# Batched decode attention with an MLP: four kv heads per K/V tile (16 KB runs), regrouped score rows, P transposed by VectorE

## Chip, core, metric

One core of a Trainium2 chip. Time is device microseconds (us) of one execution, the median of several runs. The kernel before takes 207.43 us (207.33 to 207.88). "Ratio" below is the mean time of a kernel's fast runs over the mean of the kernel before's fast runs of the same rounds, so it is not quite the quotient of the medians quoted beside it. A run over 1.5% above the fastest of its kernel counts as slow and is left out of ratios.

## The reference, cut to what matters

```
# A: one decode step, B=8, D=512, 32 q heads, 8 kv heads, window W=2048 of 8192 keys, Dh=128, bf16
q = (layernorm(x) @ wq)                                # wq: 512 x 4096
k, v = k_cache[:, :, Sk-W:, :], v_cache[:, :, Sk-W:, :] # [b, head] -> 2048 x 128, 4 q heads share one
o = softmax(q k^T * Dh**-0.5) v
h = x + o @ wo                                         # wo: 4096 x 512
# B: a second layernorm, a residual MLP (w3: 512 x 1792, w4: 1792 x 512, gelu); S=1 makes its token shift zero
out = h + B(layernorm(h))
```

K and V of the window are 64 pieces of 512 KB each, one per batch and kv head: together 67.1 MB of the 79.2 MB that the program reads. Each byte is used for very little arithmetic, so I expected the transfer from memory to be the limit; the page below shows it as such (DMA engines over 90% busy, 408 GB/s).

With the given inputs the attention term `o @ wo` has a root mean square of 6.6e-5 beside 1.05 for the output. A comparison of outputs can therefore not see an error in the attention. So the programs were also executed functionally, off the chip, on larger inputs (K, V and wq times 20, wo times 157) whose attention term is 0.30.

## The kernel before

K and V of one (batch, kv head) are one transfer of 512 KB. Partition `p` gets rows `16p` to `16p+15`, a contiguous run of 4 KB:

```python
NC = W // 128                                   # 16 rows per partition
knat = sb([128, NK, NC * DH], dt.bfloat16, "knat")   # 15 slots; vnat: 16 slots
...
e.dma_start(knat[:, ks, :].rearrange("p (c d) -> p c d", c=NC),
            A_k_cache[b, g, W0:SK, :].rearrange("(p c) d -> p c d", c=NC)).then_inc(sem_k[ks], 16)
```

TensorE transposes K in 128x128 pieces into PSUM, ScalarE and VectorE copy halves to SBUF (`Elo`, `Ehi`), TensorE forms scores (rows: 32 heads in each of four key quarters), and per batch P is transposed by four TensorE transposes and one VectorE copy. Then PV:

```python
for q in range(4):
    for jt in range(4):
        c = 4 * q + jt
        ins = e.matmul(misc[:, OT4.start + q*H + R*g : OT4.start + q*H + R*(g+1)],
                       vnat[:, vs, c*DH:(c+1)*DH], pT_sb[:, b % 2, c, R*g:R*(g+1)],
                       start=(jt == 0), stop=(jt == 3))
```

All transfers go through SyncE's one queue: x, wq (4 MB), K and V interleaved, wo, w3, w4.

## Time and profile before

| | before | view |
|---|---|---|
| DMA engines busy | over 90% in nearly all slices up to 200 us | forty slices |
| rate, 40 to 160 us | 408 GB/s | table by stretches |
| TensorE busy | 78% of the span | first part of the page |
| end | last weights land at 200.0 us, then 3.3 us of matmuls | chain of waits |

Lines of the page of the kernel before. Each digit of the PEclk and DMA rows, and each number of the GB/s row, is one fortieth of the span; the packets line says how many packets the transfers became:

```profile
span 205.6 us, 6282 instructions
PE 161.1 (78%) x2744; PEld 123.5 (60%) x2744; DVE 83.4 (41%) x197; ACT 81.8 (40%) x101; POOL 3.0 (1%) x13
...
PEclk9999997975997599769696969579969588885556
DMA  6999999999999999999999999999999999999980
GB/s 206 440 388 416 409 408 410 409 408 407 405 411 408 407 410 409 406 409 410 406 410 406 408 409 410 407 406 408 409 406 408 410 410 381 356 393 340 398 305 22
DMA packets 24250, 79.59 MB, mean 387 GB/s; under 512 B 2192, under 2 KB 6304, under 8 KB 24096
...
q1 hardware_dynamic: 24224, 79.19, 97.9%
```

The DMA row is full and flat at about 408 GB/s: the stream is the limit. The count "under 512 B 2192": these are the 4-byte packets (2192 records, median 9 ns) that go with a transfer's landing, 16 for each K or V transfer. I read them as one for each engine that the transfer used, because the packets in flight agree: 16.3 on average between 40 and 160 us here.

The table by stretches (one row, 40 to 160 us: busy us of each engine and its instructions, granted clock, DMA share, GB/s):

```profile
40.00:160.00 120.00, 104.59 (x1741) 80.65 (x1740) 54.82 (x122) 52.37 (x62) 0.00 (x0) 0.83 1.03 408
```

The end of the chain of waits (start us, duration us, what):

```profile
187.19 12.79 DMA knat<-in_B_w_dram
199.98 0.14 issue
200.12 3.30 PE b L689 x28
```

### The profile page before, as it was taken

To read this page: it belongs to the slowest core of one execution; us is meant where nothing else is said; L and a number is where in the kernel's file an instruction comes from. 1 tells how busy PE (TensorE), PEld (TensorE's weight loads), DVE (VectorE), ACT (ScalarE), POOL (GpSimd) and SP (SyncE) were. 2 spreads that over 40 slices of the span, in tenths; PEclk is the share of its full clock that TensorE was granted. 3 is DMA by queue.
4 is the path that set the end of the run, shared out by engine and by line. 5 is a ranking of instruction groups with operands and counts; after the bars stand their busy time and mean duration, and the time that the engine had idled before them with its cause. 6 is when DMAs were issued, how large, how long until landed. Compare 5 with 4: busy or idle time off the path is not lost.

```text
span 205.6 us, 6282 instructions
## 1 busy us (share of the span) xinstructions
PE 161.1 (78%) x2744; PEld 123.5 (60%) x2744; DVE 83.4 (41%) x197; ACT 81.8 (40%) x101; POOL 3.0 (1%) x13
## 2 busy tenths in 40 slices
PE   1039957799779977995899699698996698775645
PEld 0039745487548754873688468575884576565542
DVE  5103534624562356234454444347345253351120
ACT  3203846514641464145523561157145341350040
POOL 5000000000000000000000000000000000000000
PEclk9999997975997599769696969579969588885556
DMA  6999999999999999999999999999999999999980
GB/s 206 440 388 416 409 408 410 409 408 407 405 411 408 407 410 409 406 409 410 406 410 406 408 409 410 407 406 408 409 406 408 410 410 381 356 393 340 398 305 22
DMA packets 24250, 79.59 MB, mean 387 GB/s; under 512 B 2192, under 2 KB 6304, under 8 KB 24096
## 3 DMA queue, kind: packets, MB, share of 16 engines
q1 hardware_dynamic: 24224, 79.19, 97.9%
q8 instruction: 22, 0.36, 0.7%
q14 instruction: 4, 0.03, 0.0%
HBM read 79.18 MB, written 0.01 MB: 385 GB/s over the span
## 4 chain that ended last, share of the span: by engine, by line
DMA 54%; SPq 24%; PE 18%; issue 2%; DVE 0%
DMA knat<-in_A_k_cache_dram 48%; SPq L239 12%; PE kT_ps L385 10%; SPq L249 7%; DMA knat<-in_B_w_dram 6%; SPq L259 4%; PE misc L523 3%; PE S_ps L415 2%; PE b L689 2%; SPq L277 1%; PE b L470 0%; PE misc L443 0%; PE b L504 0%; PE misc L475 0%; DVE out_sb L699 0%
## 5 line engine op out<-in xcount | busy, mean ns | idle before, releaser
L396 ACT ACTIVATE kT_sb<-kT_ps 128x1024 bf16<-128x1024 bf16 x64 | 65.4, 1023 | 87.7 <-PE kT_ps L385 87.6
L385 PE MATMUL kT_ps<-ident_b,knat 128*128 128x128 bf16 x1024 | 84.6, 249 | 19.6 <-DMA knat<-in_A_k_cache_dram 18.6
L385 PEld LDWEIGHTS kT_ps<-ident_b,knat 128*128 128x128 bf16 x1024 | 72.4, 113 | 36.9 <-DMA knat<-in_A_k_cache_dram 27.8
L403 DVE COPY kT_sb<-kT_ps 128x1024 bf16<-128x1024 bf16 x64 | 44.2, 691 | 61.9 <-PE kT_ps L385 61.9
L523 PE MATMUL misc<-pT_sb,vnat 128*128 128x4 bf16 x1024 | 29.0, 165 | 3.1 <-issue 1.6
L523 PEld LDWEIGHTS misc<-pT_sb,vnat 128*128 128x128 bf16 x1024 | 27.4, 98 | 6.6 <-issue 4.2
L415 PE MATMUL S_ps<-kT_sb,qblk 128*32 128x512 bf16 x256 | 29.0, 446 | 0.3 <-DVE kT_sb L403 0.3
L415 PEld LDWEIGHTS S_ps<-kT_sb,qblk 128*32 128x32 bf16 x256 | 6.6, 95 | 8.8 <-issue 3.3
L357 PE MATMUL S_ps<-xlnT,wbig 128*128 128x8 bf16 x128 | 3.6, 168 | 6.5 <-DMA wbig<-in_A_wq_dram 6.5
L436 ACT ACTIVATE P_sb<-S_ps,negmcol 128x512 bf16<-128x512 f32 x8 | 5.5, 687 | 7.2 <-DVE negmcol L428 7.2
L533 DVE TENSOR_TENSOR prod_sb<-misc,w_sb 128x128 f32<-128x128 f32 x8 | 2.3, 292 | 14.7 <-PE misc L523 14.7
L509 DVE COPY w_sb<-b 128x128 f32<-128x128 f32 x8 | 2.3, 292 | 13.5 <-PE b L504 13.5
L357 PEld LDWEIGHTS S_ps<-xlnT,wbig 128*128 128x128 bf16 x128 | 3.5, 104 | 6.5 <-issue 6.5
L426 DVE TENSOR_REDUCE mcol<-S_ps 128x1 f32<-128x512 f32 x8 | 5.5, 682 | 0.6 <-PE S_ps L415 0.6
L581 ACT ACTIVATE std<-var,eps_t 128x8 f32<-128x8 f32 x1 | 0.3, 301 | 12.4 <-DVE var L632 12.4
L373 DVE TENSOR_SCALAR qblk<-S_ps 128x32 bf16<-128x32 f32 x8 | 0.9, 182 | 9.8 <-PE S_ps L357 9.8
L504 PE MATMUL b<-w_row,ones_row 1*128 1x128 f32 x16 | 4.7, 385 | 0.0
L460 ACT ACTIVATE a_row<-d_row 1x128 f32<-1x128 f32 x8 | 2.5, 306 | 5.7 <-DVE d_row L453 5.7
L443 PE MATMUL misc<-ident_f,mcol 128*1 128x128 f32 x16 | 3.8, 328 | 1.0 <-DVE negmcol L428 1.0
L599 PE MATMUL S_ps<-oT_all,wbig 128*128 128x8 bf16 x128 | 3.7, 168 | 0.7 <-DMA wbig<-in_A_wo_dram 0.7
L599 PEld LDWEIGHTS S_ps<-oT_all,wbig 128*128 128x128 bf16 x128 | 3.6, 104 | 0.8 <-DMA wbig<-in_A_wo_dram 0.8
L659 PE MATMUL misc<-uT,knat 128*128 128x8 bf16 x56 | 1.7, 168 | 2.7 <-DMA knat<-in_B_w_dram 2.7
(78 smaller groups left out, 70.0 us busy)
## 6 DMA issues: line engine op xcount, KB each, us to landing
knat<-in_A_k_cache_dram SPq DMA_DIRECT2D x64, 512.0 KB, 15.6
vnat<-in_A_v_cache_dram SPq DMA_DIRECT2D x64, 512.0 KB, 15.8
wbig<-in_A_wq_dram SPq DMA_DIRECT2D x1, 4096.0 KB, 12.3
wbig<-in_A_wo_dram SPq DMA_DIRECT2D x1, 2048.0 KB, 19.9
knat<-in_B_w_dram SPq DMA_DIRECT2D x1, 1792.0 KB, 12.3
wbig<-in_A_wo_dram SPq DMA_DIRECT2D x1, 1024.0 KB, 12.3
wbig<-in_A_wo_dram SPq DMA_DIRECT2D x2, 512.0 KB, 11.2
knat<-in_B_w_dram SPq DMA_DIRECT2D x1, 1024.0 KB, 12.8
```

What stands on the lines that cost most here:

```text
L239: e.dma_start(vnat[:, vs, :].rearrange("p (c d) -> p c d", c=NC), A_v_cache[b, g, W0:SK, :].rearrange("(p c) d -> p c d", c=NC),).then_inc ...
L249: e.dma_start(knat[:, ks, :].rearrange("p (c d) -> p c d", c=NC), A_k_cache[b, g, W0:SK, :].rearrange("(p c) d -> p c d", c=NC),).then_inc ...
L259: e.dma_start(wo_v[:, h0:h1, :], A_wo[h0 * 128:h1 * 128, :].rearrange("(h p) n -> p h n", p=128)).then_inc(sem_wo[j], 16)
L357: ins = e.matmul(S_ps[:, 0, h * B:(h + 1) * B], wq_v[:, kc, h * DH:(h + 1) * DH], xlnT[:, kc * B:(kc + 1) * B], start=(kc == 0), stop=(kc ...
L385: ins = e.matmul(buf[:, c * 128:(c + 1) * 128], knat[:, ks, c * DH:(c + 1) * DH], ident_b[:, :], is_transpose=True)
L396: e.activation(kT_sb[:, i % NKT, 0:W // 2], kT_ps[i % 2][:, 0:W // 2], ACT.Copy).then_inc(sem_Elo, 1)
L403: e.tensor_copy(kT_sb[:, i % NKT, W // 2:W], kT_ps[i % 2][:, W // 2:W]).then_inc(sem_Ehi, 1)
L415: ins = e.matmul(S_ps[32 * q:32 * (q + 1), b % 2, :], qblk[:, b, g, :], kT_sb[:, i % NKT, 512 * q:512 * (q + 1)], start=(g == 0), stop=(g ...
L426: ins = e.tensor_reduce(mcol[:, j:j + 1], S_ps[:, j, :], AX.X, ALU.max)
L436: e.activation(P_sb[:, j, :], S_ps[:, j, :], ACT.Exp, bias=negmcol[:, j:j + 1], scale=1.0, accum_out=lcol[:, j:j + 1]).then_inc(sem_exp, 1)
L523: ins = e.matmul(misc[:, OT4.start + q * H + R * g:OT4.start + q * H + R * (g + 1)], vnat[:, vs, c * DH:(c + 1) * DH], pT_sb[:, b % 2, c, ...
L599: ins = e.matmul(hT_ps[:, k * B:(k + 1) * B], wo_v[:, h, k * 128:(k + 1) * 128], oT_all[:, h, :], start=False, stop=(h == H - 1), skip_gro ...
```

## The change

The intent: longer runs. A tile now holds four kv heads, each on 32 partitions with 64 rows (16 KB) per partition; 33 transfers, most of 2 MB, replace 128. The ten slots lie on a 512-byte boundary (`pad`). Score rows are grouped by head, so that a 32x32 transpose on VectorE puts P directly into a block-diagonal tile, with which one PV matmul serves four heads.

```diff
+GL = 4
+PP = 128 // GL          # 32 partitions per head
+C = W // PP             # 64 rows per partition
+        pad = sb([128, 384], dt.uint8, "pad")
+        slots = sb([128, NS, C * DH], dt.bfloat16, "slots")   # NS = 10
-        knat = sb([128, NK, NC * DH], dt.bfloat16, "knat")
-        vnat = sb([128, NV, NC * DH], dt.bfloat16, "vnat")
 ...
-                    knat[:, ks, :].rearrange("p (c d) -> p c d", c=NC),
-                    A_k_cache[b, g, W0:SK, :].rearrange("(p c) d -> p c d", c=NC),
-                ).then_inc(sem_k[ks], 16)
+                    src = cache[b, GL * gq:GL * (gq + 1), W0:SK, :].rearrange("g (p c) d -> g p (c d)", c=C)
 ...
+                        e.dma_start(dst, src).then_inc(sem_slot[slot], 16)     # dst = slots[:, slot, :]
 ...
+        def dve_pT(e, b):       # replaces four TensorE transposes and a copy
+            for gl in range(GL):
+                rows = slice(32 * gl, 32 * (gl + 1))
+                ins = e.transpose(pT_sb[rows, j, :, rows], P_sb[rows, j, :].rearrange("r (c p) -> r c p", p=PP))
 ...
+                ins = e.matmul(ot[:, :, o:o + R], slots[:, slot, c * DH:(c + 1) * DH], pt[:, cc, :, o:o + R],
+                               start=(c == 0), stop=(cc == CC - 1), skip_group_check=True)
```

(Cut: the same regrouping in QK and in the softmax rows, slots shared by K, V and the weights, the order of issue.)

## The prediction

> **What bounds the kernel now.** The DMA stream. The page of forty slices shows the DMA engines at 90% or more until 200 us of the 205.6 us span, at 406 to 411 GB/s between 13 and 170 us (the table by stretches). TensorE is busy 78% of the span; from 40 to 160 us it is busy 87% at a mean granted clock of 0.83, and still waits 28 us in all for K tiles (the waits). VectorE 41% and ScalarE 40% have slack. The chain of waits ends with the last weight load, landed at 200.0, then 3.3 us of final matmuls and the store.
>
> **What one packet costs.** The trace's DMA packet records, by size, give medians on one of 16 engines: 1 KB 47 ns, 2 KB 84, 3.5 KB 140, 4 KB 160 (16,384 of them, all of K and V), 32 KB 1220 (the wq load; undisturbed 1213). All fit 9 ns + bytes / 27.2 GB/s. [...] Each transfer adds one semaphore packet per engine, 9.5 ns.
>
> **What changes.** K and V move as 4,096 packets of 16 KB. Estimate from the fit: 611 ns a packet; eight and a semaphore are 4.90 us per 2 MB tile, 428 GB/s, against 1.29 us per 512 KB, 407 GB/s (measured 408). 67.1 MB then take 157 us instead of 164.5: about 7.5 us less, all on the critical path, since the queue is full throughout. Slot alignment adds little I can see: 4 KB packets pay no more overhead than others. The wq load had the same kind of addressing [...] and ran clean, so I expect no HBM penalty [...].
>
> Off the path, if TensorE keeps up:
> - TensorE per batch: four P transposes (0.33 us) go; the 1,024 PV matmuls (27 ns apart at full clock) get 16 moving columns for 4[...]. QK reads 64-byte pieces; I expect 0.33 to 0.40 us as now. Full-clock work is about 15.5 us per batch, 18.7 at clock 0.83; a batch of data arrives every 19.6 us instead of 20.5. Tight, but ten 2 MB slots decouple it.
> - VectorE per batch: the 0.42 us copy goes; four 32-block transposes of 512 columns come[...].
> - Start: the first K tile lands near 19.5 us; K transposes start there instead of 17.0. Harmless.
> - Tail: wo, w3, w4 unchanged; their slots are free early. After the last V only 2.9 us of slack lies before w3, and the V piece is now 1 MB: at most +0.7 us.
>
> **Prediction: 200.3 us** (0.966 of before), 8 in 10 between 198.0 and 204.5. Faster by over 2%: 0.85; within 2%: 0.12; slower: 0.03.
>
> **What would show it.** Right: 16 KB packets near 612 ns, 425 to 429 GB/s mid-kernel without dips, last landing near 192.5 us, TensorE busy 90% there[...]. Wrong: packets well above 620 ns (a memory conflict); or slices where the DMA share drops, the DMA queue waiting on K transposes or PV: then TensorE under its throttled clock is the new limit; or final matmuls waiting for PV and projection instead of w4.
>
> **What would make it wrong.** TensorE's clock falling further as its work is compressed; dearer strided QK or PV matmuls; [...] a longer half-clock tail (0.5 from 184 us on).

The sum of the forecast: 207.4 us less 7.5 for the shorter stream is 199.9; the 0.4 us up to 200.3 are not broken down there. The 15.5 us of full-clock work per batch agree with the trace of the kernel before: eight groups of 16 K transposes (1.00 us each), eight of QK (0.33), two of PV (1.69), and about 1.4 us of the rest are 15.4.

## The result, and the profile after

The changed kernel takes **698.84 us** (692.33 to 707.43), ratio 3.357, 95% interval 3.327 to 3.388; the run of 707.43 counts as slow. The prediction was 200.3.

The same lines of the page of the changed kernel:

```profile
span 699.9 us, 6148 instructions
PE 173.5 (25%) x2712; PEld 133.4 (19%) x2712; DVE 107.9 (15%) x221; ACT 80.5 (11%) x101; POOL 8.0 (1%) x14
...
PEclk9997665655656565655656565656556565565555
DMA  6222222222222222222222222222222226222436
GB/s 261 63 77 98 109 110 109 109 106 109 110 108 108 109 103 109 110 107 108 109 110 109 108 107 109 108 110 109 108 108 110 108 112 168 107 77 85 126 123 222
DMA packets 10174, 79.57 MB, mean 114 GB/s; under 512 B 277, under 2 KB 4389, under 8 KB 5797
...
q1 hardware_dynamic: 10148, 79.18, 28.8%
```

The computing engines do about the same work as before and wait. The waits (engine, line waited for: us in total, times, longest) name the K and V tiles:

```profile
PEld kT_ps L379 <- DMA slots<-in_A_k_cache_dram: 288.8, 16, 31.1
PE kT_ps L379 <- DMA slots<-in_A_k_cache_dram: 285.5, 16, 31.0
PE misc L527 <- DMA slots<-in_A_v_cache_dram: 220.2, 17, 32.6
```

The DMA queue's own waits show SyncE waiting for K transposes (157.8 us, and 32.6 before wo) and PV (42.2 us), which looks like slots freed too late. But at 20 to 60 us the rate was already only 75 GB/s, with tiles queued that need no freed slot.

The end of its chain; the tail itself is as long as before:

```profile
681.84 12.39 DMA slots<-in_B_w_dram
694.23 0.14 issue
694.36 3.30 PE b L694 x28
```

Two things in the trace say what happened before any experiment. First, the DMA packet records: the 16 KB packets of K and V have a median of 611 ns, exactly what was predicted, but between 35 and 560 us only 4.02 packets are in flight on average, against 16.3 before (40 to 160 us). Four engines at 16,384 bytes per 611 ns are 107 GB/s. Second, the semaphore packets. Before: 138 transfers on 16 engines, less 8 each for the two 8-row transfers of x and out, make 128 x 16 + 8 x 16 + 8 + 8 = 2192, the page's count. After: 33 K and V transfers on 4 engines, 8 of weights on 16, and x and out on 8 each make 33 x 4 + 128 + 16 = 276; the trace holds 276 on that queue, and the page's 277 has one other small packet.

The median hides one thing. Between 20 and 40 us the packets' median is 1,002 ns, and between 40 and 60 us a quarter take over 928; from 80 to 560 us nearly all are at 611, and after 560 us a fifth are slow again. This is why the rate at 20 to 60 us was 75 and not 107 GB/s. Estimate from the packet records: the time above 611 ns adds up to 123 us on four engines, about 30 us of the 699. The cause was not tested.

### The profile page after: what moved, and what is told of

Same layout as the page of the kernel before. It is cut to its first block, busy times and chain, and to the rows that moved or that the text cites. A ratio compares the mean times of both kernels' runs of the same rounds, so it can differ in the third digit from the quotient of the medians.

```text
span 699.9 us, 6148 instructions
## 1 busy us (share of the span) xinstructions
PE 173.5 (25%) x2712; PEld 133.4 (19%) x2712; DVE 107.9 (15%) x221; ACT 80.5 (11%) x101; POOL 8.0 (1%) x14
## 4 chain that ended last, share of the span: by engine, by line
another core or an unknown queue 57%; PE 21%; DMA 15%; SPq 6%; issue 0%; DVE 0%
PE kT_ps L379 12%; DMA slots<-in_A_v_cache_dram 7%; DMA slots<-in_A_k_cache_dram 7%; SPq L260 6%; PE misc L527 4%; PE S_ps L411 3%; DMA slots<-in_B_w_dram 2%; PE b L503 1%; PE b L694 0%; PE misc L461 0%; PE misc L481 0%; DVE xln_b L704 0%; SPq L234 0%; SPq L235 0%
## 5 line engine op out<-in xcount | busy, mean ns | idle before, releaser
L379 PE MATMUL kT_ps<-ident_b,slots 128*128 128x128 bf16 x1024 | 94.4, 267 | 285.5 <-DMA slots<-in_A_k_cache_dram 285.5
L379 PEld LDWEIGHTS kT_ps<-ident_b,slots 128*128 128x128 bf16 x1024 | 81.5, 123 | 306.6 <-DMA slots<-in_A_k_cache_dram 288.8
L527 PE MATMUL misc<-pT_sb,slots 128*128 128x16 bf16 x1024 | 30.0, 174 | 220.2 <-DMA slots<-in_A_v_cache_dram 220.2
L527 PEld LDWEIGHTS misc<-pT_sb,slots 128*128 128x128 bf16 x1024 | 28.7, 104 | 225.0 <-issue 121.8
L411 PE MATMUL S_ps<-kT_sb,qstrip 128*32 128x512 bf16 x256 | 30.3, 491 | 0.0
L445 DVE STREAM_TRANSPOSE pT_sb<-P_sb 32x512 bf16<-32x512 bf16 x32 | 22.4, 700 | 0.3
L411 PEld LDWEIGHTS S_ps<-kT_sb,qstrip 128*32 128x32 bf16 x256 | 6.1, 98 | 7.8 <-issue 4.3
L294 DVE TENSOR_SCALAR ident_f<-prod_sb 128x128 f32<-128x128 f32 x1 | 7.1, 7136 | 1.5 <-POOL prod_sb L210 1.5
L295 DVE TENSOR_SCALAR ident_b<-prod_sb 128x128 bf16<-128x128 f32 x1 | 7.1, 7060 | 0.0
L503 PEld LDWEIGHTS b<-w_row,ones_row 1*128 1x128 f32 x16 | 4.0, 308 | 0.2
```

Source lines behind the costliest of these rows:

```text
L294: e.tensor_single_scalar(ident_f[:], iota_f[:], 0.0, ALU.is_equal)
L295: e.tensor_single_scalar(ident_b[:], iota_f[:], 0.0, ALU.is_equal).then_inc(sem_dveP, 1)
L379: ins = e.matmul(kT_ps[i % 2][:, c * 128:(c + 1) * 128], slots[:, slot, k0:k0 + DH], ident_b[:, :], is_transpose=True)
L411: ins = e.matmul(S_ps[32 * gl:32 * (gl + 1), b % 2, :], qstrip[:, b, GL * gq + gl, o:o + 32], kv[:, gl, :, :], start=(gq == 0 and qi == 0) ...
L445: ins = e.transpose(pT_sb[rows, j, :, rows], P_sb[rows, j, :].rearrange("r (c p) -> r c p", p=PP))
L503: e.matmul(b6[:, WBC], ones_row[0:1, :], w_row[0:1, (b % 2) * 128:(b % 2 + 1) * 128], start=True, stop=True).then_inc(sem_wbc, 1)
```

## The experiments

Three theories were stated before the first run. **Theory 1:** the source's access pattern now has the head, a count of 4, as its outermost dimension, and such a transfer runs on only 4 of the 16 DMA engines. The traces at hand fit it: 4 semaphore packets for each K or V transfer of the changed kernel, 8 for the 8-row transfers of x and out, 16 for a K or V transfer of the kernel before, whose outermost dimension is 128. **Theory 2:** reading four heads 2 MB apart conflicts in memory. **Theory 3:** the large slots are freed too late.

### e1: the kernel before with an outermost dimension of 4

```diff
-                    A_k_cache[b, g, W0:SK, :].rearrange("(p c) d -> p c d", c=NC),
+                    A_k_cache[b, g, W0:SK, :].rearrange("(p o c) d -> o p (c d)", o=4, c=NC),
```

(The same for V; the destination is `knat[:, ks, :]`. Attention doesn't depend on the order of the keys, so the result stays right.)

> The kernel before with one thing changed: in the K and V transfers the rows are dealt to the partitions so that the source's outermost dimension counts 4 (packets stay 4 KB, result stays right). Theory 1 (a transfer whose source's outermost dimension counts 4 runs on 4 of the 16 DMA engines): 32 packets of 160 ns and a semaphore per 512 KB, 5.13 us each, 657 us for 128 of them, in all 680 to 700 us, about 4 packets in flight, about 100 GB/s. Theory 2 (reading four heads 2 MB apart at once conflicts in HBM) and theory 3 (2 MB slots are freed too late and the queue starves): no heads are mixed and the slots are those of before, so 207 us.

Measured: 686.14 us in one run; packets median 159 ns, 95th percentile 161; 4.1 packets in flight between 40 and 160 us; 656 semaphore packets = 128 x 4 + 128 + 16. Its page:

```profile
DMA  6222222222222222222222222222222222227266
GB/s 271 105 106 105 105 106 106 105 105 105 105 106 106 105 104 106 106 105 105 106 106 107 105 105 105 107 104 105 105 106 106 106 105 105 106 106 177 102 183 227
```

One rearranged access pattern, in K and in V, makes the old kernel about as slow as the new one, with its own packets, slots and engines' work. Theory 1 holds; theories 2 and 3 expected 207.

### e8: the same with an outermost dimension of 8

The edit is that of e1 with `o=8`.

> As the run of the kernel before with outermost dimension 4, now 8. Theory 1: 8 engines, 8 packets in flight, and if packets keep 160 ns 16 of them and a semaphore per 512 KB, 2.57 us, 329 us for all K and V and 355 to 370 us in all. If the engines then collide as in the run with 16, packets of 240 ns and more, and 450 us or more. Theories 2 and 3: 207 us.

Measured: 394.80 us in one run, and 1168 semaphore packets = 128 x 8 + 144: eight engines. The time is above the range for free packets and below that for colliding ones, and the trace shows why: between 20 and 100 us packets have medians of 186 to 205 ns with a quarter above 248 to 261, from 120 to 340 us the median is 159 and the 95th percentile at most 167, and between 340 and 360 us the median is 262. So the slow packets that the next run shows are here too, at the beginning and at the end. Its GB/s row:

```profile
GB/s 321 216 153 157 157 156 157 162 162 163 168 206 210 211 207 210 210 208 210 211 210 211 211 210 209 213 209 209 208 208 206 212 209 211 227 204 205 215 352 104
```

### e2: the same with an outermost dimension of 16

The edit is that of e1 with `o=16`.

> As the run before, but the outermost dimension counts 16. Theory 1: 16 engines again, 207 us within 1%, which also shows that dealing out the rows costs nothing. Theories 2 and 3: 207 us as well.

Measured: 281.56 us (267.79 to 309.73, four runs that differ too much among themselves for a ratio; three count as slow, among them the profiled one of 285.00, and even the fastest is 29% above the kernel before). This is a miss of theory 1 as I had put it. The DMA share is full and the semaphore packets are those of 16 engines (2192), but 4 KB packets have a median of 240 ns, and the rate begins at 244 GB/s and creeps up to 320. With fewer engines the rate was lower (105 GB/s between 40 and 160 us in e1, 181 in e8), but here it is 265 with all 16, against 408 in the kernel before: the number of engines alone does not give the rate.

```profile
GB/s 283 364 244 241 244 247 243 245 246 250 257 253 252 253 255 259 264 264 289 293 292 301 307 310 324 319 321 321 318 311 314 313 320 315 278 283 281 334 373 58
```

### e3: the changed kernel with the row blocks outermost

```diff
-.rearrange("g (p c) d -> g p (c d)", c=C)
+.rearrange("g (p c) d -> p g (c d)", c=C)
```

The partition order becomes `4p + g`, so the later matmuls mix heads: wrong. Functional execution on larger inputs shows the error (1.48 root mean square, against 0.0045 for the changed kernel). Everything else, slots and waits included, is the changed kernel.

> The changed kernel with the source of K and V taken with the 32 row blocks outermost and the 4 heads inside (heads then alternate over the partitions, so the result is wrong on purpose; every instruction and size is the same). Theory 1: 16 engines, 16 packets in flight, 425 to 429 GB/s, and the time of the prediction, 198 to 203 us. Theory 2: all four heads are still read at once, so the rate stays near 110 GB/s and the time near 700 us. Theory 3: slots are freed as before, near 700 us.

Measured: 198.74 us (198.53 to 198.91), ratio 0.9579 (0.9565 to 0.9593). 672 semaphore packets = 33 x 16 + 144.

```profile
span 196.8 us, 6148 instructions
...
PEclk9999999958995799699859995899696966955555
DMA  6999999999999999999999999999999999999980
GB/s 215 426 416 426 423 433 426 433 436 430 421 433 426 426 426 435 426 423 430 430 433 430 426 425 416 440 430 430 426 440 426 426 382 391 421 399 326 403 345 20
DMA packets 10569, 79.57 MB, mean 404 GB/s; under 512 B 672, under 2 KB 4784, under 8 KB 6192
...
L445 DVE STREAM_TRANSPOSE pT_sb<-P_sb 32x512 bf16<-32x512 bf16 x32 | 22.4, 701 | 0.3
```

and its row of the table by stretches, beside which TensorE's busy time and clock are those of before:

```profile
40.00:160.00 120.00, 105.93 (x1772) 81.74 (x1772) 71.35 (x145) 53.17 (x66) 0.00 (x0) 0.84 1.01 428
```

The whole loss of the changed kernel is the order of two dimensions in one access pattern.

### e4 and e5: one transfer per head, and where it writes

e4 keeps the changed kernel's layout and result, and issues a tile as four transfers of 32 partitions each:

```diff
-                        e.dma_start(dst, src).then_inc(sem_slot[slot], 16)
+                        for gl in (0, 2, 1, 3):
+                            e.dma_start(dst[PP * gl:PP * (gl + 1), :], src[gl]).then_inc(sem_slot[slot], 16)
```

> The changed kernel with each tile's transfer cut into four, one per head (32 partitions, outermost dimension 32), issued in the order of heads 0, 2, 1, 3; right result. Theory 1: 16 engines; if the 32 partitions of one transfer take writes as fast as 128 do, 199 to 204 us[...]. Theories 2 and 3: near 700 us.

Measured: 319.16 us (305.09 to 326.97; three of the four runs count as slow, among them the profiled one of 322.80, and the fastest is 47% above the kernel before). All 16 engines work (2256 semaphore packets = 33 x 4 x 16 + 144), but 16 KB packets take 1108 ns in the median, and the trace shows 226 GB/s between 40 and 160 us and 269 between 200 and 300 us. So the case of 199 to 204 us did not come.

e5 leaves those reads as they are and writes each head to every fourth partition (wrong, as e3):

```diff
-                            e.dma_start(dst[PP * gl:PP * (gl + 1), :], src[gl]).then_inc(sem_slot[slot], 16)
+                            e.dma_start(dst[gl::GL, :], src[gl]).then_inc(sem_slot[slot], 16)
```

> As the run with one transfer per head, with the same reads in the same order, but each head's 32 rows are written to every fourth partition (over all 128) instead of to 32 neighbours; result wrong on purpose. If the 32-partition transfers were slow [...]: 16 KB packets return to about 611 ns and the time to 198 to 204 us. If the reads were what conflicted (16 engines at once in one head of 512 KB): packets stay near 1100 ns and the time near 320 us.

Measured: 198.96 us in one run, packets 611 ns. The GB/s rows of e4 and then of e5:

```profile
GB/s 312 331 219 221 227 223 229 215 227 222 229 223 223 225 225 228 229 236 233 237 235 241 247 241 255 261 255 262 266 274 294 286 294 267 274 268 234 268 403 88
```

```profile
GB/s 215 426 416 429 429 426 423 429 426 432 424 426 429 432 426 423 423 429 432 423 429 423 423 434 429 429 423 429 419 423 439 426 386 390 410 394 380 414 317 25
```

Only the destination differs, so what slows e4's packets (1108 ns against 611) lies on the write side. Whether e2's slow packets (240 ns) and e8's (medians of 186 to 205) have the same cause was not tested. Blocks of neighbouring partitions alone are not enough: e1's transfers also go to four blocks of 32 neighbouring partitions, and its packets are not slow (median 159 ns, 95th percentile 161). A rate that creeps up during the run is what both e2 (244 GB/s between 20 and 60 us, 317 between 180 and 240) and e4 (223 between 20 and 60, 269 between 200 and 300) show.

### e6: a right version with all engines

To keep e3's transfer and the right result, the block-diagonal P has to follow the partition order `4p + g`:

```diff
+            ... .rearrange("g (p c) d -> p g (c d)", c=C)                     # as e3
-                               ident_b[:, :], is_transpose=True)              # K transposes
+                               perm_b[:, :], is_transpose=True)               # puts columns back in (g p) order
-            e.activation(P_sb[:, j, :], S_ps[:, j, :], ACT.Exp, ...)
+            e.activation(P_sb[:, 0, :].rearrange("r (u g) -> r u g", g=GL), rep4, ACT.Exp, ...)  # each P four times
-                ins = e.transpose(pT_sb[rows, j, :, rows], P_sb[rows, j, :]...)
+                    ins = e.matmul(pT_ps[:, o*128:(o+1)*128], P_sb[:, 0, c*128:(c+1)*128], ident_b[:, :], is_transpose=True)
+                e.tensor_tensor(pT_sb[:, 0, CR*r:CR*(r+1), :], pT_ps..., mask, ALU.mult)  # two rounds of 8 pieces
```

The mask is 4 where the partition's head is the column's head and 0 elsewhere; the 4 undoes the fourfold sum that the softmax's accumulator now holds. P and pT have one buffer each instead of two.

> A right version of the run with outermost dimension 32: heads alternate over partitions; the K transposes use a permutation matrix for the identity, exp writes each probability four times over, and TensorE transposes P in 16 pieces per batch that VectorE masks into the block-diagonal tile. Theory 1: 16 engines at about 427 GB/s. TensorE gets 12 more transposes per batch than before (about 0.8 us at full clock) and so about 16.5 us of full-clock work per 19.6 us of data: between 198 and 204 us, 200 in the middle; if TensorE falls behind, slices of the DMA below 420 GB/s and up to 207 us.

Measured: 198.84 us (198.81 to 198.98), ratio 0.9590 (0.9577 to 0.9603): faster than both kernels.

```profile
span 196.8 us, 6416 instructions
...
DMA  6999999999999999999999999999999999999990
GB/s 215 426 413 436 423 426 423 426 426 433 431 426 433 430 425 426 426 436 423 426 433 426 433 426 428 423 423 430 430 426 433 443 378 385 416 403 328 397 362 24
```

TensorE did not fall behind: its extra transposes (10.7 us busy in all) fit beside a full stream. Its granted clock was 0.89 to 0.90 in all four runs, where e3 had 0.82 to 0.84 with TensorE busy about as long (154.2 and 155.6 us); why stays open. On the larger inputs its functional execution agrees with the reference as closely as the kernel before does (0.0046 for both). On the chip only the output comparison was made, which cannot see the attention.

### e7, e9 to e12: where the buffers start

The prediction dismissed the alignment of the slots. The buffers of the kernel before start 384 bytes past a 512-byte boundary, the slots after start on one. Each of these runs changes only the size of a pad.

```diff
-        pad = sb([128, 384], dt.uint8, "pad")
+        pad = sb([128, 416], dt.uint8, "pad")      # e7, on top of e3; e11: 256
+        pad = sb([128, 128], dt.uint8, "pad")      # e9, new in the kernel before; e10: 32, e12: 384
```

> The run with outermost dimension 32, with the pad 32 bytes longer, so that every slot starts 32 bytes past a 512-byte boundary. The prediction said that alignment adds little: the same ratio as that run, 0.958 within 0.003, 16 KB packets of 611 ns. Rival, that the aligned slots are part of the gain: 1% or more slower, packets above 617 ns.

> The kernel before with 128 bytes of padding ahead of its tensors, so that its K, V and weight buffers start on a 512-byte boundary (before: 384 bytes past one). If a start that is a multiple of 128 already is clean: 207.4 us, ratio 1.000 within 0.003. If the offset of 384 costs the 3 to 4 ns a packet that an offset of 32 was seen to cost with long packets, 1,024 packets per engine for K and V and the tail give it back: 203 to 205 us, and part of the intended gain is alignment, not run length.

> The kernel before with 32 bytes of padding, so that the buffers start on an odd multiple of 32. With 3 to 4 ns a packet, 1,024 K and V packets per engine and some 1.2 us in the tail: 211 to 213 us, ratio 1.017 to 1.027. If alignment matters for long packets alone: 207.4 us.

> The run with outermost dimension 32 with slots 384 bytes past a 512-byte boundary, as the buffers of the kernel before lie. If a multiple of 128 is clean: ratio 0.958 within 0.003, as with aligned slots. If only 512 is clean: up to 0.973, as with the offset of 32.

> The kernel before with 384 bytes of padding, so that the buffers start on an odd multiple of 256. If a multiple of 256 is what a packet's destination needs [...]: as the run on a 512-byte boundary, ratio 0.975 within 0.003, 4 KB packets 159 ns at the 95th percentile. If 512 is needed: 1.000, as with the offsets of 384 and 416.

| run | base | start, mod 512 | us | ratio (95%) | K/V packet ns, median / 95th percentile / mean |
|---|---|---|---|---|---|
| before | | 384 | 207.46 | 1 | 160 / 171 / 163.1 |
| e10 | before | 416 | 207.65 | 1.0008 (0.9994 to 1.0021) | 162 / 168 / 163.4 |
| e12 | before | 256 | 202.68 | 0.9768 (0.9754 to 0.9781) | 159 / 159 / 159.9 |
| e9 | before | 0 | 202.25 | 0.9754 (0.9741 to 0.9768) | 159 / 159 / 159.9 |
| e7 | e3 | 32 | 201.82 | 0.9734 (0.9721 to 0.9747) | 614 / 621 / 618.6 |
| e11 | e3 | 384 | 201.01 | 0.9693 (0.9680 to 0.9706) | 612 / 621 / 617.7 |
| e3 | | 0 | 198.74 | 0.9579 (0.9565 to 0.9593) | 611 / 611 / 614.4 |

e7 and e10 are misses of the main expectation: e7 was to show no effect, e10 a loss to 211 us or more. e10 came out at its alternative's time, but not for that reason (long packets alone): e9 shows that the 4 KB packets of the kernel before already pay. e9 was even faster than its range of 203 to 205. A start at 0 or 256 (159.9 ns in the mean) is clean, one at 384, 416 or 32 costs about 3 to 4 ns a packet: 3.2 and 3.5 for 4 KB packets (384, 416), 4.2 and 3.3 for 16 KB packets (32, 384; 256 was not run with these). Why these starts differ the runs do not show. For the 4 KB packets the cost is the larger share (3.2 of 159.9 ns against 3.3 of 614.4 at a start of 384), so it touches the old layout most. The GB/s row of the kernel before on an aligned start (e9):

```profile
GB/s 211 418 409 416 420 416 420 416 419 418 412 419 419 419 417 418 415 417 420 414 419 418 417 421 417 418 415 418 414 414 421 419 421 402 376 397 347 398 367 32
```

Between 40 and 160 us it moves 417 GB/s, where the kernel before moves 408 and e3 428.

## Why the prediction was wrong, point by point

- **The failed step.** "Estimate from the fit: 611 ns a packet; eight and a semaphore are 4.90 us per 2 MB tile, 428 GB/s." The packet was right (median 611 ns). "Eight" was not: a tile's 128 packets fell on 4 engines, 32 each, 19.6 us a tile and 107 GB/s by the same arithmetic (109 measured). I took 16 engines for granted, because all K and V transfers of the kernel before used 16. The diff showed the outermost dimension of 4, and the trace of the kernel before held a sign that a transfer can use fewer engines, the 8 semaphore packets of an 8-row transfer; I used neither. e1 shows the outermost count of 4 by itself (656 semaphore packets, 686.14 us), e8 another count (1168, 394.80 us), e3 that undoing it gives the predicted time back. The prediction's own sign for trouble, a falling DMA share with the queue waiting for K transposes or PV, was to mean that TensorE is the limit; it came (share 0.25, 157.8 and 42.2 us) with TensorE busy 25% of the span.
- **The guard didn't help.** I considered a memory conflict from the addresses and dismissed it. It was not the cause of the loss (most packets stay at 611 ns), though the slow packets at both ends, about 30 us by the estimate above, stay unexplained. And among the things that "would make it wrong" there was no way of losing engines. A chance of 0.03 for slower was far too sure.
- **"The queue is full throughout"** was right for e3 and e6 and not enough after the change: tiles were queued, but with 4.02 packets in flight about twelve of the 16 engines moved nothing (DMA share 0.25).
- **"Slot alignment adds little I can see"** was wrong. Aligning the old kernel alone gives 207.46 to 202.25, 5.2 us; longer runs and the rest of the rewrite on top (e3) bring it to 198.74, 3.5 us more. So the run length, on which I put all 7.5 us, is worth less than half of the available gain of 8.7. The sign was in the records: I read medians (160 ns), where the spread (159 to 171, mean 163.1) was the cost. Two errors hid it: with that mean the fit gives 399 GB/s for the kernel before, not 407, and the 16.3 packets in flight on 16 engines, a little overlap that the fit leaves out, bring it back to about the measured 408.
- **"If TensorE keeps up"** it does: in e3 it was busy 105.9 of 120 us at clock 0.84, before 104.6 at 0.83, and the stream stayed at 428 GB/s.
- **Small terms**, read in e3: VectorE transposes 0.70 us; the first K transposes start at 18.45 us, estimated 19.5; the last weights land at 191.2 us, estimated 192.5; PV pieces of 64 matmuls with 16 columns take 1.69 to 1.86 us in the chain of waits, where those of the kernel before with 4 columns take 1.69 to 1.70, so the extra columns cost at most 0.17 us a piece there.
- **The time of 200.3 us** was thus a fair estimate of a kernel (e6) that the change was not, and in part by luck: it gave 7.5 us to run length, which brought 3.5 at most, and nothing to alignment, which brought 5.2.

## What to carry to other kernels

Read a transfer's source pattern for its outermost dimension (4 gave 4 engines here, 8 gave 8, 16, 32 and 128 gave 16) and its destination for the partitions that it covers (32 neighbours gave 1108 ns a packet in e4, every fourth of 128 gave 611 in e5), and check the semaphore packets or the packets in flight in the trace: the changed kernel on 4 engines looked like slow memory (109 GB/s), though most of its packets were as fast as predicted (611 ns). Look at the spread of packet times as well as at the median, and at where buffers that receive large streams start: here 0 and 256 bytes past a 512-byte boundary gave 202.25 and 202.68 us, 384 gave 207.46. A rewrite that brings several changes should be split by experiments even when it wins: here 5.2 of the 8.7 us to be had were one line of padding.
